# The integer additions of the weight conversion in a two-layer kernel: on GpSimd or on VectorE

## Chip, cores and metric

The kernel runs on one core of a Trainium2 chip. The metric is the device time of one execution in microseconds (us), from the first to the last instruction and what lies around them. TensorE (PE in the profile, PEld for its weight loads), VectorE (DVE), ScalarE (ACT), GpSimd (POOL) and SyncE (SP, which issues most transfers) run side by side; each works through its own instructions in the order in which they stand, and semaphores make one wait for another.

## What is computed

An attention block over 2 x 768 tokens, a dense layer with an ELU between two matrix products, and a mixture of eight experts of which each token takes one. The change touches only the dense layer, which the code calls the first layer:

```python
def _moe_ref(x, w_in, w_out):            # x: 1536 x 512, w_in: 512 x 2048, w_out: 2048 x 512
    h = x @ w_in
    alpha = 1.0
    g = np.where(h > 0.0, h, alpha * (np.exp(np.minimum(h, 0.0)) - 1.0))
    return (g @ w_out).astype(np.float32)
```

`w_in` and `w_out` are handed to the kernel as 64-bit words (the bits of doubles), and the kernel itself makes 32-bit floats of them.

## The kernel before

**Tiling.** The 1536 tokens stand in 4 blocks of 512, 256, 384 and 384 (index `j`), and the 2048 hidden columns in 16 slices of 128 (index `c`, `NF = 16`). For each block and slice PE makes `h` (`mm_h`, L422: 12 matmuls, because each product of 128 x 128 is taken three times: upper half by upper half, upper by lower, lower by upper), ACT and DVE make the ELU of it (`elu`: ACT L433 to L435, DVE L436 and L437), ACT and DVE split the result into an upper and a lower half (`split_g`: ACT L447, DVE L448), and PE adds its share to `y` (`mm_y1`, L467). In block 0 the slices below `C3 = 8` take one full float32 product for `y` (rows `y<-wo,elp`); from slice 8 on it is three products of halves (`y<-wsp,gh` and `y<-wsp,gl`), which needs the weight's halves, from ACT L175 and DVE L176.

**The conversion** of one weight slice goes over three engines. DVE shifts and masks the upper words into the tile `cv_t` (`conv_t`, L138 and L139), ACT scales the lower words into `cv_r` (`conv_r`, L127), and `conv_f` (L146) adds the two as 32-bit integers: in place into `cv_t` for `w_in`, into `wo` for `w_out`. There are 32 slices (16 of `w_in`, 16 of `w_out`), so 32 such additions, all on GpSimd before. For `w_in` the result is then split: ACT rounds the upper half (`conv_h`, L152), and `conv_l` (L157) subtracts it to give the lower half `wi`. The table `LOE` puts slices 3, 9 and 15 of these subtractions on GpSimd and the other 13 on DVE.

**Attention beside it.** While block 0 runs through its slices, the attention of the tokens of block 1 is made in units of 64 tokens: scores on PE (L309), maximum on DVE (L319, L324), exponentials on ACT (L336), normalisation on DVE (L353, L354, L361), a transpose on PE (L371), a copy on ACT (L378), the product with the values on PE (L392), and its halves on ACT (L398) and DVE (L405). Transpose and product use one PSUM bank, `T`, of which there is only one: the transpose of the next unit waits until L405 of the unit before has read it.

**What sets the order.** Up to the first slices of block 0 the order is written out by hand (`START`, run by `start_up`): there `A`, `B` and `C` with a slice and a 0 (`w_in`) or 1 (`w_out`) are the conversion's three steps, `D` and `E` the halves. `START` holds seven of the 32 additions and the subtractions of slices 0 to 3. The rest comes from a loop over blocks and slices (in `part1`) with two conversions to each slice; there the Tile framework's own scheduler sets the order of the instructions on every engine. The tiles `cv_t` and `cv_r` come from one pool of 5 buffers (`stg`), the raw `w_out` slices from one of 4 (`ws`), so later loads wait for earlier conversions.

Of the kernel before, what the change touches and what calls it, by code (L numbers as in the profile page):

```python
# [9 lines left out]
F32 = mybir.dt.float32  # L10
# [5 lines left out]
ALU = mybir.AluOpType  # L16
# [40 lines left out]
EXD = (3, 5)  # L57
EXP = (0, 1, 2, 3, 4, 6, 7)
NORMD = (0, 4, 7)
LOE = "VVVPVV"  # L60
START = "w23 w43 x3 w53 w03 w13 w33 w51 x1 w31 w21 w11 w41 w01 w52 x2 w22 w02 w12 w42 w50 x0 w00 w20 w32 d2 d0 w40 d5 k2 s0 w30 d3 k4 k1 k3 s2 k0 k5 m0 w10 s5 m2 e0 s3 m5 M0 e2 m3 d4 M1 r0 b5 d1 b3 s4 n0 e5 r2 t0 e3 m4 n2 s1 c0 z3 e4 M2 z5 t2 r3 r5 M3 n3 c2 m1 A00 M4 n5 B00 e1 M5 k6 r4 C00 n4 t5 P s6 r1 c5 p1 n1 A01 p6 t4 p2 D0 o5 B01 c4 o2 h5 k7 m6 t3 C01 h2 s7 c3 E0 e6 t1 p7 m7 p0 A10 r6 o0 c1 p3 n6 p4 e7 o3 l5 B10 o1 t6 h3 r7 h0 C10 l3 c6 n7 o4 A11 l0 h1 t7 B20 h4 o6 A20 c7 l1 C20 h6 l4 o7 D1 l2 l6 H0 h7 E1 D2 l7 A30 B30 E2 C30 H1 B11 C11 D3 A21 B21 E3 C21"
HID = (5, 10, 15)
LOP = (1, 3, 5, 8, 10, 12, 14)
# [16 lines left out]
class Prog:  # L80
# [60 lines left out]
    def conv_f(self, c, part):  # L141
        t2, r = self.cv.pop((c, part))
        f = t2
        if part == 1:
            f = self.wo[:, c].bitcast(I32)
        self.nc.gpsimd.tensor_tensor(f, t2, r, op=ALU.add)  # L146
        self.w[c, part] = f

    def conv_h(self, c):
# [4 lines left out]

    def conv_l(self, c):
        w, f = self.w[c, 0], self.cvf.pop(c)
        (self.nc.gpsimd if LOE[c % len(LOE)] == "P" else self.nc.vector).tensor_tensor(w[:, 1], f, w[:, 0].bitcast(F32), op=ALU.subtract)  # L157

    def conv_a(self, c, part):
        self.conv_r(c, part)  # L160
# [376 lines left out]
    def part1(self):  # L537
# [31 lines left out]
        for x in ORDER.split():  # L569
            f = dict(q=self.load_q, n=self.load_v0, v=self.load_v, w=wload, k=self.load_k0, c=self.load_c)[x[0]]  # L570
            f(int(x[1:]))
        self.new_x(0)
        self.new_x(1)
        self.start_up()
        conv_done = [x for x in pieces if x in self.w]
        del cq[:len(conv_done)]
        while dq and dq[0] in self.split:
# [66 lines left out]
        for i in range(len(steps)):  # L644
            run(2 * i)
            j, c = steps[i]
# [19 lines left out]
    def start_up(self):  # L666

        unit = dict(d=self.diag_q, k=self.k_sum, s=self.scores, m=self.maxes, b=self.less_max, e=self.at1b, z=self.sums, r=self.recip, n=self.norm,
                    t=self.turn, c=self.turned, o=self.weighted, h=self.x_hi, l=self.at5, p=self.v_pad, x=self.max_k0, M=self.mean_v0)
        part = dict(A=self.conv_r, B=self.conv_t, C=self.conv_f)  # L670
        self.split, self.half = set(), set()
        with self.tc.manual_schedule():
            for op in START.split():
                if op[0] == "H":
                    self.mm_h(0, int(op[1:]), 0, TB // 2)
                    self.half.add(int(op[1:]))
                    continue
                k, n = op[0], [int(i) for i in op[1:]]
                if k in unit:
                    unit[k](*n)  # L680
                elif k in part:
                    part[k](*n)
                    if k == "C" and n[1] == 1:
                        self.split.add((n[0], 1))
                elif k == "w":
                    self.window(*n)
                elif k == "P":
                    self.pad_v0()
                elif k == "D":
                    self.conv_h(*n)  # L690
                elif k == "E":
                    self.conv_l(*n)
                    self.split.add((n[0], 0))
# [805 lines left out]
```

## Time and profile before

| | us |
|---|---|
| median of 3 runs (567.41 to 567.75) | 567.46 |
| the profiled execution | 567.08 |
| its span | 565.3 |
| PE busy over the span | 538.3 (95%) |
| DVE busy | 366.3 (65%) |
| ACT busy | 311.4 (55%) |
| POOL busy | 115.7 (20%) |

The profile's times start at the first instruction of the profiled execution; around its span lie 1.8 us more. Matmuls overlap in their records, so a matmul's cost is the distance between starts, not its duration. PEclk is the granted clock of TensorE as a share of 2.4 GHz. A DVE instruction's record also overlaps the next one's by about 0.08 us.

### The profile page before, as it was taken

The page shows a single profiled execution, that of the slowest core. Times are in us where ns is not written, and L with a number is a line of the kernel's source. Part 1 is how long each engine was busy: PE and PEld are TensorE (multiplying, and loading weights), DVE is VectorE, ACT ScalarE, POOL GpSimd, SP SyncE. Part 2 cuts the span into 40 slices and gives each one's busy share as a digit, 9 for nine tenths or more (in the row PEclk, how much of TensorE's full clock was granted, in tenths as well). Part 3 has the DMA queues.
Part 4 walks back from the last instruction along what each step waited for, and adds up shares of the span by engine and source line. Part 5 has one row for each costly group of instructions (what it writes and reads, how often), then busy time and mean ns, then how long its engine had stood idle before and what let it go on. Part 6 is the DMA issues. An engine that isn't in the chain of part 4 may idle for free. (4 is left out here: it accounts for less than half of the span.)

```text
span 565.3 us, 9614 instructions
## 1 busy us (share of the span) xinstructions
PE 538.3 (95%) x3113; PEld 422.5 (75%) x3113; DVE 366.3 (65%) x966; ACT 311.4 (55%) x768; POOL 115.7 (20%) x139
## 2 busy tenths in 40 slices
PE   8877998789999999999999999999999999999995
PEld 4465664557889888988888989877888665675884
DVE  6999899997647886787565778885741100444510
ACT  5775564546557877775665754673232222565620
POOL 3656365434000000000000000431432111100001
PEclk9979999889999999999999999998999999999999
DMA  9999733342114130310100101541077979593611
GB/s 291 317 353 399 239 139 105 123 133 52 57 48 138 49 93 16 118 48 14 48 2 1 56 1 50 170 118 56 19 221 267 382 260 370 162 379 131 237 56 40
DMA packets 38714, 81.33 MB, mean 144 GB/s; under 512 B 4095, under 2 KB 8575, under 8 KB 38656
## 3 DMA queue, kind: packets, MB, share of 16 engines
q1 hardware_dynamic: 36336, 73.30, 38.8%
q0 software_dynamic: 2320, 7.34, 3.8%
q8 instruction: 26, 0.43, 0.3%
q14 instruction: 32, 0.26, 0.1%
HBM read 103.70 MB, written 6.55 MB: 195 GB/s over the span
## 5 line engine op out<-in xcount | busy, mean ns | idle before, releaser
L422 PE MATMUL h<-xh,wi 128*128 128x384 f32 (+2 forms) x528 | 144.6, 342 | 0.2 <-ACT elp L435 0.2
L467 PE MATMUL y<-wsp,gh 128*128 128x512 f32 x320 | 100.9, 403 | 0.3
L422 PEld LDWEIGHTS h<-xh,wi 128*128 128x128 f32 x528 | 93.6, 189 | 8.3 <-ACT elp L435 1.0
L422 PE MATMUL h<-xl,wi 128*128 128x384 f32 (+2 forms) x264 | 88.0, 333 | 0.0
L467 PEld LDWEIGHTS y<-wsp,gh 128*128 128x128 f32 x320 | 58.2, 191 | 10.5 <-ACT gh L447 1.1
L467 PE MATMUL y<-wsp,gl 128*128 128x512 f32 x160 | 62.3, 405 | 1.3 <-DVE gl L448 1.3
L1157 DVE TENSOR_TENSOR holdl<-S,holdh 128x512 fp32r<-128x512 f32 x22 | 15.2, 689 | 72.1 <-ACT holdh L1153 53.7
L1125 PE MATMUL h<-w2s,holdh 128*128 128x512 f32 x176 | 61.0, 407 | 0.0
L1168 PE MATMUL y<-w2s,holdh 128*128 128x512 f32 x176 | 59.1, 398 | 0.0
L436 DVE SCALAR_TENSOR_TENSOR elt<-ele,elt 128x384 f32<-128x384 f32 (+2 forms) x64 | 41.3, 646 | 19.5 <-ACT ele L434 19.1
L422 PEld LDWEIGHTS h<-xl,wi 128*128 128x128 f32 x264 | 49.9, 189 | 4.5 <-issue 1.2
L433 ACT ACTIVATE elt<-h 128x384 f32<-128x384 f32 (+2 forms) x64 | 31.4, 491 | 28.5 <-PE h L422 23.0
L447 ACT CAST gh<-elp 128x384 fp32r<-128x384 f32 (+2 forms) x56 | 27.8, 496 | 31.9 <-DVE elp L437 22.0
L176 DVE TENSOR_TENSOR wsp<-wo,wsp 128x512 fp32r<-128x512 f32 x56 | 39.9, 713 | 8.2 <-ACT wsp L175 7.5
L437 DVE SCALAR_TENSOR_TENSOR elp<-elt,elp 128x384 f32<-128x384 f32 (+2 forms) x64 | 41.8, 652 | 3.9
L175 ACT CAST wsp<-wo 128x512 fp32r<-128x512 f32 x56 | 34.7, 620 | 15.4 <-PE y L467 13.8
L1125 PEld LDWEIGHTS h<-w2s,holdh 128*128 128x128 f32 x176 | 33.9, 192 | 8.3 <-issue 0.8
L336 ACT ACTIVATE e<-e,nb 128x120 f32<-128x120 f32 x88 | 33.7, 389 | 10.4 <-DVE nb L324 10.2
L1168 PEld LDWEIGHTS y<-w2s,holdh 128*128 128x128 f32 x176 | 33.1, 188 | 8.4 <-issue 1.6
L448 DVE TENSOR_TENSOR gl<-elp,gh 128x384 fp32r<-128x384 f32 (+2 forms) x56 | 31.0, 554 | 12.1 <-ACT gh L447 10.8
L467 PEld LDWEIGHTS y<-wsp,gl 128*128 128x128 f32 x160 | 29.9, 190 | 8.4 <-DVE gl L448 2.5
L1125 PE MATMUL h<-w2s,holdl 128*128 128x512 f32 x88 | 35.0, 398 | 0.0
(290 smaller groups left out, 973.1 us busy)
## 6 DMA issues: line engine op xcount, KB each, us to landing
wo<-in_w SPq DMA_DIRECT2D x9, 2048.0 KB
wo<-in_w SPq DMA_DIRECT2D x18, 1024.0 KB
ri<-in_w_in SPq DMA_DIRECT2D x16, 512.0 KB
ro<-in_w_out SPq DMA_DIRECT2D x16, 512.0 KB
wo<-in_w SPq DMA_DIRECT2D x32, 256.0 KB
w2p<-in_w SPq DMA_DIRECT2D x32, 256.0 KB
w2q<-in_w SPq DMA_DIRECT2D x24, 256.0 KB
q<-in_q SPq DMA_DIRECT2D x18, 256.0 KB
```

Of the source, the lines that this page charges most:

```text
L175: nc.scalar.copy(w[:, 0], f)
L176: nc.vector.tensor_tensor(w[:, 1], f, w[:, 0].bitcast(F32), op=ALU.subtract)
L336: nc.scalar.activation(e[:, p], e[:, p], AF.Exp, bias=nb[:, p:p + 1], scale=0.125, accum_out=sm[:, p:p + 1])
L422: nc.tensor.matmul(h, lhsT=w[:, wl, k * 128:k * 128 + 128], rhs=x[:, k, a:b], start=(n == 0), stop=(n == 11))
L433: nc.scalar.activation(t, h, AF.Tanh, scale=0.5)
L436: nc.vector.scalar_tensor_tensor(t, e, 1.0, t, op0=ALU.add, op1=ALU.mult)
L437: nc.vector.scalar_tensor_tensor(p, t, 0.0, p, op0=ALU.min, op1=ALU.add)
L447: nc.scalar.copy(gh, p)
L448: nc.vector.tensor_tensor(gl, p, gh.bitcast(F32), op=ALU.subtract)
L467: nc.tensor.matmul(self.y[j][t], lhsT=gx[:, sl], rhs=wx, start=(c == 0 and n == 0), stop=(c == NF - 1 and n == len(ops) - 1))
L1125: nc.tensor.matmul(self.h[s, hf], lhsT=x[:, k], rhs=w, start=(n == 0), stop=(n == 11))
L1168: nc.tensor.matmul(self.y2[s], lhsT=g[:, ks], rhs=w, start=(i == 0 and n == 0), stop=(i == 7 and n == 2))
```

## The change

The table `LOE` goes, and `conv_l` always stands on VectorE. `conv_f` asks a flag, `self.early`, that is set while `start_up` runs and cleared behind it: the seven additions of `START` stay on GpSimd, the other 25 go to VectorE. The subtractions of slices 3 (in `START`), 9 and 15 go to VectorE too. So 28 instructions move.

```diff
@@ -57,7 +57,6 @@
 NORMD = (0, 4, 7)
-LOE = "VVVPVV"
...
@@ -143,7 +142,7 @@
         f = t2
         if part == 1:
             f = self.wo[:, c].bitcast(I32)
-        self.nc.gpsimd.tensor_tensor(f, t2, r, op=ALU.add)
+        (self.nc.gpsimd if self.early else self.nc.vector).tensor_tensor(f, t2, r, op=ALU.add)
         self.w[c, part] = f
...
     def conv_l(self, c):
         w, f = self.w[c, 0], self.cvf.pop(c)
-        (self.nc.gpsimd if LOE[c % len(LOE)] == "P" else self.nc.vector).tensor_tensor(w[:, 1], f, w[:, 0].bitcast(F32), op=ALU.subtract)
+        self.nc.vector.tensor_tensor(w[:, 1], f, w[:, 0].bitcast(F32), op=ALU.subtract)
...
@@ -572,6 +571,7 @@
         self.start_up()
+        self.early = False
         conv_done = [x for x in pieces if x in self.w]
...
@@ -668,7 +668,7 @@
-        self.split, self.half = set(), set()
+        self.split, self.half, self.early = set(), set(), True
```

Since one line goes, L60 to L571 of the kernel before are one lower in the changed one: its L145 is L146 here. The scheduler also sets many instructions behind `start_up` in another order, on PE, DVE, ACT and SP. Three places follow.

GpSimd, from the end of `START` on, before (`cv_t` and `wo` are additions, `wi_655` is the lower half of slice 3, L297 copies key maxima for the attention, L709 prepares routing constants):

```order
L709 CAST wg_668<-r_wg_670 128x4x16
L146 TENSOR_TENSOR cv_t<-cv_t,cv_r 128x512
L146 TENSOR_TENSOR wo<-cv_t,cv_r 128x512
L157 TENSOR_TENSOR wi_655<-cv_t,wi_655 128x512
L146 TENSOR_TENSOR wo<-cv_t,cv_r 128x512
L297 COPY k<-ks_96 128x96
```

and in the changed kernel:

```order
L709 CAST wg_668<-r_wg_670 128x4x16
L145 TENSOR_TENSOR cv_t<-cv_t,cv_r 128x512
L145 TENSOR_TENSOR wo<-cv_t,cv_r 128x512 x2
L296 COPY k<-ks_96 128x96 x2
L296 COPY k<-ks_97 128x96 x12
L1199 TENSOR_TENSOR w2s<-wo,w2s 128x512 x3
```

Behind the additions of `START` no conversion is left on GpSimd; only the small copies of L297 stand there until the experts' weights.

VectorE around the first ELU instructions of block 0, before:

```order
L437 SCALAR_TENSOR_TENSOR elp<-elt,elp 128x512
L138 TENSOR_SCALAR cv_t<-ri_701 128x512
L324 TENSOR_SCALAR nb<-mx 128x4
L139 SCALAR_TENSOR_TENSOR cv_t<-ri_701,cv_t 128x512
L436 SCALAR_TENSOR_TENSOR elt<-ele,elt 128x512
L437 SCALAR_TENSOR_TENSOR elp<-elt,elp 128x512
```

and in the changed kernel:

```order
L137 TENSOR_SCALAR cv_t<-ri_701 128x512
L436 SCALAR_TENSOR_TENSOR elp<-elt,elp 128x512
L145 ISA wo<-cv_t,cv_r 128x1024
L323 TENSOR_SCALAR nb<-mx 128x4
L138 SCALAR_TENSOR_TENSOR cv_t<-ri_701,cv_t 128x512
L435 SCALAR_TENSOR_TENSOR elt<-ele,elt 128x512
L145 ISA cv_t<-cv_t,cv_r 128x1024
```

The additions stand between the conversion's first step and the ELU. On VectorE they have another form: a custom instruction (ISA) that sees the same 512 words of a partition as 1024 elements of two bytes.

TensorE at the end of `h` of slice 8 (`wi_1013`) and at the turn of an attention unit, before:

```order
L422 MATMUL h<-xl_202,wi_1013 128x512
L371 MATMUL T<-c_128,e 120x128 x4
L422 MATMUL h<-xh_201,wi_1013 128x512
L309 MATMUL S<-k,q 128x120 x4
L467 MATMUL y<-wo,elp 128x512 x4
```

and in the changed kernel:

```order
L421 MATMUL h<-xl_202,wi_1013 128x512
L421 MATMUL h<-xh_201,wi_1013 128x512
L308 MATMUL S<-k,q 128x120 x4
L370 MATMUL T<-c_128,e 120x128 x4
L466 MATMUL y<-wo,elp 128x512 x4
```

The transpose into the bank `T` (L371) stands two steps later, behind the scores of the next unit.

## Rows read from the trace of the kernel before

**Rows 1.** The page's head.
```profile
span 565.3 us, 9614 instructions
```

**Rows 2.** Windows: length, busy us (instructions) by engine, PEclk, DMA share, GB/s.
```profile
47.07:140.37 93.30, 81.11 (x348) 53.24 (x346) 87.07 (x152) 52.34 (x119) 45.30 (x33) 0.95 0.48 160
140.37:200.00 59.63, 59.63 (x432) 52.40 (x431) 41.11 (x116) 40.77 (x116) 2.42 (x5) 1.00 0.24 77
200.00:300.00 100.00, 100.00 (x702) 89.44 (x701) 72.02 (x245) 68.41 (x202) 1.73 (x5) 1.00 0.14 43
```

**Rows 3.** Waits of PE, 47.07 to 140.37: total us, times, longest.
```profile
PE T L371 <- DVE xl L405: 5.5, 2, 4.4
PE y L467 <- DVE elp L437: 3.2, 1, 3.2
PE y L467 <- DVE gl L448: 1.3, 1, 1.3
PE T L392 <- ACT et L378: 1.1, 1, 1.1
```

**Rows 4.** Timeline of PE: start, us, instruction, [idle before <- releaser].
```profile
53.24 5.37 PE L467 MATMUL y<-wo,elp 128*128 128x512 f32 x8 [3.16 <-DVE elp L437]
...
61.21 3.59 PE L467 MATMUL y<-wo,elp 128*128 128x512 f32 x8
...
101.28 0.65 PE L371 MATMUL T<-c,e 128*120 128x128 f32 x4 [4.40 <-DVE xl L405]
```

**Rows 5.** Timeline of POOL.
```profile
93.26 1.27 POOL L146 TENSOR_TENSOR cv_t<-cv_t,cv_r 128x512 int32<-128x512 int32 x1 [0.72 <-DVE rr L353]
94.48 1.48 POOL L157 TENSOR_TENSOR wi<-cv_t,wi 128x512 fp32r<-128x512 f32 x1
```

**Rows 6.** Timeline of DVE at the same time.
```profile
93.30 1.51 DVE L138 TENSOR_SCALAR cv_t<-ro 128x512 int32<-128x512 int32 x1
94.73 1.75 DVE L361 TENSOR_TENSOR e<-e,rr 128x480 f32<-128x480 f32 x1
```

**Rows 7.** DVE groups, 47.07 to 140.37: xcount | busy us, mean ns | idle before.
```profile
L437 DVE SCALAR_TENSOR_TENSOR elp<-elt,elp 128x512 f32<-128x512 f32 x12 | 14.4, 1202 | 0.5
L157 DVE TENSOR_TENSOR wi<-cv_t,wi 128x512 fp32r<-128x512 f32 x10 | 12.7, 1267 | 0.0
L436 DVE SCALAR_TENSOR_TENSOR elt<-ele,elt 128x512 f32<-128x512 f32 x12 | 12.5, 1045 | 0.8 <-ACT ele L434 0.6
...
L139 DVE SCALAR_TENSOR_TENSOR cv_t<-ri,cv_t 128x512 int32<-128x512 int32 x12 | 9.8, 818 | 0.0
L138 DVE TENSOR_SCALAR cv_t<-ro 128x512 int32<-128x512 int32 x13 | 9.5, 734 | 3.2 <-POOL wi L157 3.2
L138 DVE TENSOR_SCALAR cv_t<-ri 128x512 int32<-128x512 int32 x12 | 5.0, 416 | 0.0
L361 DVE TENSOR_TENSOR e<-e,rr 128x480 f32<-128x480 f32 x4 | 4.8, 1193 | 0.0
```

**Rows 8.** DVE groups, 200 to 300, where GpSimd is nearly idle.
```profile
L176 DVE TENSOR_TENSOR wsp<-wo,wsp 128x512 fp32r<-128x512 f32 x23 | 15.9, 689 | 3.6 <-ACT wsp L175 3.3
...
L361 DVE TENSOR_TENSOR e<-e,rr 128x480 f32<-128x480 f32 x8 | 5.2, 656 | 0.2
...
L448 DVE TENSOR_TENSOR gl<-elp,gh 128x256 fp32r<-128x256 f32 x9 | 3.8, 422 | 0.7 <-ACT gh L447 0.6
```

**Rows 9.** POOL groups, 47.07 to 140.37.
```profile
L146 POOL TENSOR_TENSOR wo<-cv_t,cv_r 128x512 int32<-128x512 int32 x14 | 20.4, 1455 | 20.8 <-DVE cv_t L139 8.6 <-ACT wi L152 4.5 <-issue 3.4
L146 POOL TENSOR_TENSOR cv_t<-cv_t,cv_r 128x512 int32<-128x512 int32 x12 | 18.9, 1578 | 20.1 <-DVE cv_t L139 8.2 <-ACT cv_r L127 5.9 <-ACT wsp L175 3.5
L157 POOL TENSOR_TENSOR wi<-cv_t,wi 128x512 fp32r<-128x512 f32 x3 | 4.5, 1506 | 0.7 <-ACT wi L152 0.7
```

**Rows 10.** Timeline of DVE while GpSimd rests.
```profile
131.79 0.68 DVE L139 SCALAR_TENSOR_TENSOR cv_t<-ri,cv_t 128x512 int32<-128x512 int32 x1
132.39 0.67 DVE L448 TENSOR_TENSOR gl<-elp,gh 128x512 fp32r<-128x512 f32 x1
```

## Prediction

> **What bounds the kernel now.** I read three views, from wide to narrow. First the windows [rows 2]: from 140 us on TensorE is busy for 59.63 of 59.63 us and then for 100.00 of 100.00, at the full granted clock of 2.4 GHz. It is the bound there, so whatever an earlier stage ends sooner arrives at the end of the kernel. The stage of 47 to 140 us, the slices 2 to 12 of the first block, is another matter: in 93.3 us TensorE is busy for 81.11, so it stands still for 12.2 us, and at a granted clock of 0.95; VectorE is busy for 87.07.
>
> Second, the waits of TensorE in that stage [rows 3]. Three of the four groups end on VectorE (5.5, 3.2 and 1.3 us); the fourth, 1.1 us, is for a ScalarE copy. GpSimd ends none of the long ones itself. In the timeline the two largest are seen singly [rows 4]: 3.16 us before the first `y` of the block, and 4.40 us before a transpose that needs the bank `T`, which VectorE's L405 had still to read. After the first wait the clock is down, too: the same product takes 5.37 us there and 3.59 us eight microseconds later.
>
> Third, why VectorE is late. At 93.26 us GpSimd starts an addition and at 94.48 a subtraction, which ends at 95.96 [rows 5]. VectorE's mask operation of 93.30 lasts 1.51 us, to 94.81, and its normalisation of 94.73 lasts 1.75, to 96.48 [rows 6], although these forms take 0.416 (mean of the undisturbed group) and 0.656 us elsewhere [rows 7, 8]. Each ends some 0.3 to 0.5 us behind GpSimd's. So a VectorE instruction that meets a GpSimd one stands until that one is done: VectorE is full, but not of its own work.
>
> **The change part by part.** *Removed from VectorE: the standing.* The cost is read from the groups of the stage against undisturbed means [rows 7, 8], 0.689 us for a form with two operands of 512 elements. L437: 12 x (1.202 - 0.689) = 6.2 us; L157: 10 x (1.267 - 0.689) = 5.8; L436: 12 x (1.045 - 0.689) = 4.3; L138 on `ro`: 13 x (0.734 - 0.416) = 4.1; L361: 4 x (1.193 - 0.656) = 2.1; L139 on `ri`: 12 x (0.818 - 0.689) = 1.5. Together 24.0 us. GpSimd has 29 conversion instructions in the stage [rows 9]; one addition of `START` stays and 28 go, so 24.0 x 28/29 = 23.2 us are freed. The copies of L297 stay and are short.
>
> *Added to VectorE: 25 additions and 3 subtractions.* A subtraction is the form of L157, which follows its predecessor at 0.60 us when nothing disturbs it, as two instructions of that size do (131.79 to 132.39) [rows 10]. The addition is not in the trace; in the changed order it is a custom form over 1024 two-byte elements. Bounds from rows: 0.60 us if it goes by bytes, since it reads and writes exactly what a subtraction of 512 words does; and if it goes by elements, (0.689 - 0.422) / 256 = 1.04 ns each [rows 8], so 0.689 + 512 x 1.04 ns = 1.22 us, less the 0.08 of overlap 1.14. I take 0.60, because L139 on `ri`, an integer form over the same tiles, costs what the float forms cost (0.68 us) [rows 10]; 1.14 is kept for a rival. Sum added: 28 x 0.60 = 16.8 us.
>
> The Trainium skill's page VectorE: DVE Perf Modes (section on the perf-mode tier table) says that `tensor_tensor` runs at one element a cycle on fp32 and at two on 16-bit operands. If the custom form follows the 16-bit row, an addition of 1024 elements takes 0.69 us by that page's figures and the sum stays as it is; if it follows the fp32 row, 1.22 us, which is the rival below. No row here shows which.
>
> *VectorE's demand* in the stage then is 87.1 - 23.2 + 16.8 = 80.7 us. The order takes some of it out: four of the 25 additions and two subtractions now stand behind the ELU of slice 11, which ended this stage before, 6 x 0.60 = 3.6 us, leaving 77.1. They fall into the window after 140 us, where VectorE has 59.6 - 41.1 = 18.5 us free [rows 2].
>
> *TensorE's demand.* Busy 81.1 us at a clock of 0.95; at the full clock 81.1 x 0.05 = 4.1 us less, 77.0. The first wait I leave where it is: the operations ahead of it lose a little standing and gain a subtraction and a mask operation. It costs 3.2 us and 5.37 - 3.59 = 1.8 us of clock. So TensorE needs 77.0 + 5.0 = 82.0 us, against 77.1 for VectorE: TensorE becomes the bound of the stage too. The transpose of the 4.40 us wait also stands later on TensorE now, behind the scores, which gives L405 more time.
>
> *What the move costs in waits.* An addition on VectorE now holds up all behind it (the next ELU, the lower halves of `x` and `g`) while it waits for ScalarE's `cv_r`. VectorE's spare of 82.0 - 77.1 = 4.9 us covers that in part, and TensorE has up to one slice of work in hand; I book 1 us of new waits. On SP the loads of raw `w_out`, of key sums and of values now wait for VectorE's additions in place of GpSimd's; they are wanted much later, and DMA is busy for 0.48 of the stage, so they cost nothing. GpSimd itself has nothing else to do there but L297.
>
> *Sum:* 93.3 - 82.0 = 11.3 us gained, less 1.0: 10.3. The profiled execution took 567.08 us for a span of 565.3 [rows 1], so around the span lie 1.8 us that do not change; the median of the runs is 0.4 us above it. From the median: 567.46 - 10.3 = 557.2 us.
>
> **The rivals.** *A, the addition goes by elements.* VectorE's demand is 87.1 - 23.2 + 25 x 1.14 + 3 x 0.60 = 94.2 us; four additions and two subtractions fall behind the stage (5.8), 88.4 are left, with 2 us of waits 90.4. VectorE stays the bound and the gain is 93.3 - 90.4 = 2.9: 564.5 us. For it: the element count in the order. Against it: the bytes. This is what the one-element-a-cycle row of the page named above would give.
>
> *B, the waits move with the work: slower.* GpSimd's waits that were not for VectorE are 4.5 + 3.4 + 5.9 + 3.5 + 0.7 = 18.0 us [rows 9]: for ScalarE, and "issue". On GpSimd they cost little; if all of them come to stand in VectorE's queue, with the 3.0 us that it idles now for others than GpSimd (93.3 - 87.1 - 3.2), the stage takes 77.1 + 3.0 + 18.0 = 98.1 us, 4.8 longer: 572.3 us. It decides from 93.3 - 77.1 - 3.0 = 13.2 us of such waits on, 0.47 us to each moved instruction. Against it: ScalarE is busy for only 52.3 of 93.3 us [rows 2], and much of its own idling is for the conversion's additions and subtractions, which come sooner now; and the scheduler sets two conversions' mask operations ahead of their additions.
>
> *C, given back later: no change.* The reordered first block ends sooner, but the left-over conversions and the ELU of block 1 then meet on VectorE and TensorE waits there for as long: 567 us. Against it: 18.5 us free for 3.6 us of work.
>
> That the change does not do what it says is no case: the changed order has no conversion on GpSimd behind `START`.
>
> **How the numbers follow.** The forecast, TensorE as the bound of the stage, gets 0.72; A 0.13; B 0.09; C 0.06. A measurement of this kernel can tell 0.2%, 1.1 us, from no change. Faster by more than that are the forecast and A, 0.85, less 0.01 for an A that comes out dearer: 0.84. Within it C, 0.06. Slower B, and the dearer A, 0.10. The range: below, the whole of TensorE's loss goes but a part of the first wait, 12.2 + 4.1 - 1.3 = 15.0 us: 552.5. Above, A's 564.5 as a whole, so that B and C alone lie outside it, 0.15.
>
> **What would show it.** Right: in 47 to 140 us the groups L437, L436 and L157 fall to means of 0.7 to 0.75 us; the additions on VectorE stand with 0.69 us; the wait for L405 is gone or under 1 us; the windows show TensorE full for the slices 3 to 12 at a clock near 1.00; slice 13 starts at 127 to 130 us and not at 140. The first wait stays near 3 us. Wrong: additions of 1.2 us (A); VectorE idle by 13 us or more with "ACT cv_r" as the releaser (B); idle TensorE between 130 and 200 us (C). The step I trust least is the 1 us of new waits: with TensorE and VectorE within 5 us of each other for the whole stage, a few badly placed instructions cost more than that.

## The result, and the profile after

The changed kernel takes **552.96 us** (median of 4 runs, 551.34 to 554.55) beside 567.43 us before (567.31 to 567.75) on the same chip: a ratio of 0.9744, 95% interval 0.9712 to 0.9775, so 14.5 us faster. Forecast were 557.2 us with a range of 552.5 to 564.5, so the time lies 4.2 us under the forecast and 0.5 us inside the range. A second comparison gave 553.17 us and 0.9747 (0.9719 to 0.9775). Ratios leave disturbed executions out, so for two of the experiments below (`e3_gpsimd_reads_again` and `e6_second_addition`) the ratio says less time than the median does, and the profile of the first, which is of a disturbed execution, is not read.

The profiled execution took 552.2 us for a span of 550.4, so 1.8 us lie around the span, as before. Line numbers from L60 to L571 are one lower than before: L435 and L436 after are L436 and L437 before, L145 is L146, L156 is L157.

To see where 14.9 us of span went I cut both traces at the same three pieces of TensorE work: up to the first product `h` of the first layer, from there to its last, and the rest. The windows of the kernel before, in the columns of [rows 2] (length, busy PE, PEld, DVE, ACT, POOL, then the granted clock):

```profile
40.25:376.35 336.10, 323.89 (x1975) 269.41 (x1974) 266.64 (x680) 214.19 (x551) 64.25 (x55) 0.98 0.29 94
376.35:565.30 188.95, 181.79 (x884) 132.21 (x883) 64.93 (x158) 69.21 (x124) 30.57 (x39) 0.98 0.56 196
```

The same of the kernel after, and below it its first layer cut once more, at the point where TensorE has as much left to do as it had before at 140.37 us (14.57 + 221.40 = 235.97 us busy, against 235.96 before):

```profile
39.54:363.15 323.61, 319.21 (x1975) 267.82 (x1973) 258.81 (x708) 215.52 (x551) 24.09 (x27) 0.99 0.30 98
363.15:550.40 187.25, 179.78 (x884) 131.13 (x883) 64.41 (x158) 68.63 (x123) 30.08 (x39) 0.99 0.56 197
...
47.07:125.80 78.73, 76.25 (x340) 50.99 (x341) 73.85 (x172) 51.11 (x117) 4.53 (x5) 0.98 0.54 181
125.80:140.37 14.57, 14.57 (x78) 12.41 (x77) 13.90 (x34) 10.66 (x27) 0.59 (x2) 1.00 0.26 84
140.37:363.15 222.78, 221.40 (x1502) 197.61 (x1501) 163.62 (x495) 149.37 (x400) 14.37 (x17) 1.00 0.19 60
```

The layer is 336.10 - 323.61 = 12.5 us shorter: TensorE's idle time in it fell from 12.2 to 4.4 us, and its busy time, on the same products, from 323.9 to 319.2 us. The layer also starts 0.7 us sooner, and the rest of the kernel is 1.7 us shorter. The stage of [rows 2] went from 93.30 to 78.73 us; VectorE's busy time in it from 87.07 to 73.85.

What TensorE still waits for, from the layer's first product to its last (total us, times, longest):

```profile
PE y L466 <- DVE elp L436: 2.5, 1, 2.5
PE y L524 <- ACT mab L511: 1.4, 1, 1.4
PE h L421 <- ACT elp L434: 0.5, 1, 0.5
```

The waits for L405 and L448 of [rows 3] are gone, the first wait, 3.2 us there, is 2.5 us here, and 1.4 us for a ScalarE copy are new, at 166 to 167 us. In the stage itself the first wait is all that is left: 78.73 - 76.25 = 2.48 us. The VectorE groups of 44 to 140 us, which answer to [rows 7]:

```profile
L138 DVE SCALAR_TENSOR_TENSOR cv_t<-ro,cv_t 128x512 int32<-128x512 int32 x15 | 11.2, 749 | 0.1
L435 DVE SCALAR_TENSOR_TENSOR elt<-ele,elt 128x512 f32<-128x512 f32 x15 | 10.4, 690 | 2.3 <-ACT ele L433 2.3
L436 DVE SCALAR_TENSOR_TENSOR elp<-elt,elp 128x512 f32<-128x512 f32 x15 | 10.3, 683 | 0.1
L145 DVE CUSTOM_DVE_ANT_0 wo<-cv_t,cv_r 128x1024 uint16<-128x1024 uint16 x13 | 8.9, 682 | 0.4 <-ACT cv_r L126 0.4
L156 DVE TENSOR_TENSOR wi<-cv_t,wi 128x512 fp32r<-128x512 f32 x13 | 8.8, 679 | 0.2 <-ACT wi L151 0.2
L137 DVE TENSOR_SCALAR cv_t<-ro 128x512 int32<-128x512 int32 x15 | 8.5, 566 | 0.0
...
L145 DVE CUSTOM_DVE_ANT_0 cv_t<-cv_t,cv_r 128x1024 uint16<-128x1024 uint16 x12 | 8.2, 680 | 0.0
```

The three groups that stood at 1202, 1045 and 1267 ns stand at 683, 690 and 679. The addition, L145, costs 0.68 us, as much as a subtraction. Its waits for ScalarE come to 0.4 us.

### The profile page after: what moved, and what is told of

Its sections match the earlier page's. It is cut to its first block, busy times and chain, and to the rows that moved or that the text cites. A ratio compares the mean times of both kernels' runs of the same rounds, so it can differ in the third digit from the quotient of the medians.

```text
span 550.4 us, 9589 instructions
## 1 busy us (share of the span) xinstructions
PE 528.4 (96%) x3113; PEld 417.6 (76%) x3113; DVE 357.8 (65%) x994; ACT 312.5 (57%) x768; POOL 74.2 (13%) x111
## 5 line engine op out<-in xcount | busy, mean ns | idle before, releaser
L466 PE MATMUL y<-wsp,gh 128*128 128x512 f32 x320 | 98.5, 398 | 0.1
L466 PE MATMUL y<-wsp,gl 128*128 128x512 f32 x160 | 60.5, 399 | 0.0
L1125 PE MATMUL h<-w2s,holdh 128*128 128x512 f32 x176 | 59.8, 400 | 0.0
L435 DVE SCALAR_TENSOR_TENSOR elt<-ele,elt 128x384 f32<-128x384 f32 (+2 forms) x64 | 37.1, 580 | 23.8 <-ACT ele L433 23.5
L436 DVE SCALAR_TENSOR_TENSOR elp<-elt,elp 128x384 f32<-128x384 f32 (+2 forms) x64 | 35.5, 554 | 3.2
L296 POOL COPY k<-ks 128x96 f32<-128x96 f32 x16 | 8.2, 516 | 199.3 <-PE S L308 137.6
L1168 PE MATMUL y<-w2s,holdl 128*128 128x512 f32 x88 | 34.4, 391 | 0.0
```

Source lines behind the costliest of these rows:

```text
L435: nc.vector.scalar_tensor_tensor(t, e, 1.0, t, op0=ALU.add, op1=ALU.mult)
L436: nc.vector.scalar_tensor_tensor(p, t, 0.0, p, op0=ALU.min, op1=ALU.add)
L466: nc.tensor.matmul(self.y[j][t], lhsT=gx[:, sl], rhs=wx, start=(c == 0 and n == 0), stop=(c == NF - 1 and n == len(ops) - 1))
L1125: nc.tensor.matmul(self.h[s, hf], lhsT=x[:, k], rhs=w, start=(n == 0), stop=(n == 11))
L1168: nc.tensor.matmul(self.y2[s], lhsT=g[:, ks], rhs=w, start=(i == 0 and n == 0), stop=(i == 7 and n == 2))
```

## The experiments

Two theories stand against each other. *Standing*: a GpSimd instruction that reads its operands holds up a VectorE instruction that reads two, so every conversion step on GpSimd costs VectorE time although it relieves it. *Relief or order*: VectorE does better for other reasons, because the planner now orders the block in another way, or because the few subtractions were badly placed. In the kernels that add work, nothing is left out: the added instructions write a scratch tile that nobody reads.

**The changed kernel once more**, beside the kernels below.

> The changed kernel once more, timed against the one before on one chip with the three kernels below. Standing theory: a gain of 13 to 15 us as measured before, with the same stage of 47 to 126 us: TensorE busy for 76 us, VectorE for 74. What is open is the granted clock of the 30 to 40 us stretch, 1.00 in the first profile of the changed kernel and 0.69 in the one before: if it was luck, it is about 0.7 here, and the first matmul of the layer starts 0.7 us later, with the total some 1 us longer.

Measured 553.17 us (551.99 to 554.93), 0.9747 (0.9719 to 0.9775). Its first layer is 324.86 us long in the profile, 1.3 more than the first trace has; so differences of 1 to 2 us between two single profiles are not explained here. The clock of 30 to 40 us is 1.00 again, not about 0.7; yet the layer starts at 40.35 us, as late as in the kernel before. So the 0.7 us by which it starts sooner in the first trace are not the change's.

**The change in two halves.** The first keeps three subtractions of the first block on GpSimd and moves only the additions; the second starts from the kernel before and moves only the subtractions.

The lines that differ in where an instruction runs:

```diff
--- after
+++ e1_additions_only
-        self.nc.vector.tensor_tensor(w[:, 1], f, w[:, 0].bitcast(F32), op=ALU.subtract)
+        (self.nc.gpsimd if c % 6 == 3 else self.nc.vector).tensor_tensor(w[:, 1], f, w[:, 0].bitcast(F32), op=ALU.subtract)
--- before
+++ e2_subtractions_only
-        (self.nc.gpsimd if LOE[c % len(LOE)] == "P" else self.nc.vector).tensor_tensor(w[:, 1], f, w[:, 0].bitcast(F32), op=ALU.subtract)
+        self.nc.vector.tensor_tensor(w[:, 1], f, w[:, 0].bitcast(F32), op=ALU.subtract)
```

> The changed kernel with the subtractions of slices 3, 9 and 15 back on GpSimd; the 25 additions stay on VectorE. Standing theory (a VectorE instruction that meets a GpSimd one stands until it is done, and that was what the change removed): three such meetings come back, about 1 us each, less 0.6 us of work each, and VectorE has spare, so 553 to 556 us. Order theory (the gain comes from the scheduler's other order of PE and VectorE): the order differs from the changed kernel's in some 200 lines on PE, so anything from 553 to 567.

> The kernel before with only the three subtractions moved to VectorE; all 32 additions stay on GpSimd. Standing theory: 3 of 28 meetings go, 2.5 us of standing against 1.8 us of added work, so 564 to 568 us, and the groups L436, L437, L157 keep means near 1.0 to 1.2 us. Order theory: the order on PE differs from that before in 251 lines, nearly as many as the changed kernel's, so a good part of the 14.5 us could come: 555 to 562.

Measured: the additions alone 554.11 us, 0.9754 (0.9714 to 0.9794), not to be told from the whole change; the subtractions alone 563.37 us, 0.9931 (0.9906 to 0.9955), 4 us, of which its profile has 2.1 us in the layer and 2.4 behind it. That is somewhat more than the standing theory gave, and the means of L435, L436 and L156 in 47 to 140 us are 828, 897 and 791 ns there, where 1.0 to 1.2 us were expected. So the additions carry the gain, and beside them the three subtractions are worth no more than the intervals leave open. Why the subtractions alone give little is in the waits of TensorE in that kernel, from 36 us on:

```profile
PE T L370 <- DVE xl L404: 3.6, 2, 3.1
PE y L466 <- DVE gl L447: 3.4, 2, 1.8
PE y L466 <- DVE nb L323: 3.2, 1, 3.2
```

VectorE still ends three long waits: 25 additions are left on GpSimd to meet it.

**GpSimd's reads put back, in the changed order.** Behind each of the 13 `w_out` additions that now run on VectorE, GpSimd makes two, or one, needless additions on the result; or, in the third kernel, six memsets, which read nothing, behind a copy of one column. The order of the other engines is the changed kernel's.

```diff
+        if part == 1 and not self.early:
+            for _ in range(2):      # e3; range(1) in e7
+                self.nc.gpsimd.tensor_tensor(self.scr, self.wo[:, c], self.wo[:, c], op=ALU.add)
```
```diff
+        if part == 1 and not self.early:      # e4
+            self.nc.gpsimd.tensor_copy(self.scr[:, :1], self.wo[:, c, :1])
+            for _ in range(6):
+                self.nc.gpsimd.memset(self.scr, 0.0)
```

> The changed kernel, with 26 needless additions on GpSimd (two behind each addition of a w_out slice; each reads 512 floats twice and writes a scratch tile that nobody reads). The order on PE, VectorE, ACT and SP is word for word the changed kernel's. Standing theory: each holds VectorE for 0.8 to 1.0 us, some 20 to 26 us in the stage of 47 to 126 us, where VectorE is busy for 73.9 of 78.7 us, so VectorE becomes the bound again: 563 to 573 us, and the means of L436, L437 and L157 (by the lines of before) rise to 0.9 to 1.2 us. Order theory: nothing waits for these instructions, so 552 to 555 us.

> The changed kernel with 13 needless additions on GpSimd, one behind each moved addition of a w_out slice; the order on PE, VectorE, ACT and SP is the changed kernel's. Standing theory: 13 meetings of 0.6 to 1.0 us, 8 to 13 us on VectorE, of which some 5 us find spare: 555 to 561 us, half of the way back to the kernel before. Order theory: 552 to 554 us.

> The changed kernel, with 78 needless memsets on GpSimd (six behind each addition of a w_out slice, behind a copy of one column), some 35 to 40 us of GpSimd's time as in the kernel before; a memset reads nothing. The order on PE, VectorE, ACT and SP is word for word the changed kernel's. Standing by GpSimd's reads: VectorE's two-operand instructions don't stand, only the one-operand mask operation (L138 of before) may, so 553 to 557 us with two-operand means near 0.69 us. Standing by whatever GpSimd runs: 563 to 573 us, as with the needless additions.

Measured ratios: 26 reads 0.9895 (0.9836 to 0.9953), 13 reads 0.9902 (0.9872 to 0.9933), 78 memsets 0.9854 (0.9797 to 0.9911). So 26 reads cost 0.0151 x 567 = 8.6 us against the changed kernel, 13 cost 8.8, and the memsets 6.2. By time alone the three don't tell reading from writing, nor one dose from two: by these ratios the 26 reads, at 561 us, stay under the range of the standing theory, the 13 reads stand at its upper end, and the memsets, at 559 us, lie above theirs. VectorE's busy time in the layer is 264.02 us with 13 reads and 261.30 with the memsets, against 258.81. But the added work brought a second thing with it, which I had not thought of: TensorE now waits for the key copies of the layer (L296 after, on GpSimd). In the kernel with 13 reads:

```profile
PE S L311 <- POOL k L299: 3.2, 1, 3.2
```
```profile
126.65 5.96 POOL L299 COPY k<-ks 128x96 f32<-128x96 f32 x2 [0.48 <-PE y L469]
```

The two copies start 0.48 us behind the needless addition ahead of them, and then they take 5.96 us, against 2.26 us for the same two in the changed kernel (from 123.56 us on), where the median of one is 0.27 us. From 126.45 to 132.28 us VectorE goes without a gap from one two-operand instruction to the next, with one mask operation among them; the copies end 0.33 us behind that. With the memsets the two copies take 3.55 us, and TensorE waits for 2.0. These three settle nothing on the time, and were done again without that wait, below.

**VectorE's spare.** The changed kernel with a second, needless addition on VectorE behind each of the 25 moved ones.

```diff
+        if not self.early:
+            self.nc.vector.tensor_tensor(self.scr, f.bitcast(F32), f.bitcast(F32), op=ALU.add)
```

> The changed kernel with a needless second VectorE addition of 512 floats (into a scratch tile) behind each of the 25 moved ones, 0.60 us each, so 15 us more work for VectorE: what an addition that goes by elements would have cost. Spare theory (the stage ends with TensorE, and VectorE, busy for 73.9 of 78.7 us, has some 4.8 us of spare): 10 us of it reach the end: 560 to 564 us. If VectorE is not near the bound at all: 553 us.

Measured 0.9949 (0.9909 to 0.999), so 0.0202 x 567 = 11.5 us more than the changed kernel, for 25 x 0.60 = 15.0 us of work. Single executions lie far apart, from 560.67 to 571.25 us; the profiled one took 568.57. Its layer:

```profile
40.12:378.37 338.25, 326.11 (x1976) 271.74 (x1973) 271.16 (x733) 215.03 (x552) 29.00 (x29) 0.97 0.29 95
```

VectorE is busy for 271.2 us, 12.4 more than in the changed kernel, and the layer is 2 us longer than in the kernel before, with 29.0 us of GpSimd's work in it where the kernel before had 64.3. So VectorE has little to spare: had an addition cost about twice 0.60 us (the first rival), most of the gain would have gone. But not all of the loss is the length of VectorE's own work. Here, too, TensorE waits for two key copies that take 6.47 us while VectorE works without a gap (from 133.39 to 139.82 us), although GpSimd has no added work in this kernel:

```profile
133.69 6.47 POOL L298 COPY k<-ks 128x96 f32<-128x96 f32 x2 [67.15 <-DVE ks L223]
```
```profile
140.00 2.06 PE L310 MATMUL S<-k,q 128*128 128x120 f32 x8 [3.35 <-POOL k L298]
```

**All of it on VectorE.** First the seven additions of `START`, then the sixteen key copies as well.

```diff
--- after
+++ e5_all_on_vector
-        (self.nc.gpsimd if self.early else self.nc.vector).tensor_tensor(f, t2, r, op=ALU.add)
+        self.nc.vector.tensor_tensor(f, t2, r, op=ALU.add)
--- e5_all_on_vector
+++ e8_key_copies_too
-            self.nc.gpsimd.tensor_copy(k[:, 0], self.ks[u // UPB])
+            self.nc.vector.tensor_copy(k[:, 0], self.ks[u // UPB])
```

> The changed kernel with the seven additions of START on VectorE too. Standing theory: seven meetings fewer before 50 us, up to 7 us of standing against 4.2 us of work, in a stretch where VectorE is busy for 9.2 to 9.9 of each 10 us; the first matmul of the layer (39.5 us) starts 0 to 2 us sooner: 551 to 553 us. Rival (the exception was needed): the additions hold up the attention's own work in VectorE's queue while they wait for ScalarE, and the layer starts 1 to 4 us later: 554 to 557 us.

> The kernel of e5_all_on_vector again, as the partner of e8_key_copies_too: 549 to 553 us.

> The kernel after with START's seven additions and the sixteen key copies (L296 there) on VectorE as well, so that GpSimd has nothing of the first layer's first block behind START. If GpSimd's remaining part still costs anything: 549 to 552 us, and no wait of TensorE on k from GpSimd. If the copies cost VectorE more than they free (16 copies of 0.2 us and a changed order): 553 to 555 us.

Measured 551.2 us (0.9716, 0.9684 to 0.9747) and, again, 551.66 us (0.9735, 0.9712 to 0.9759) for the first, which the intervals don't set apart from the changed kernel. With the key copies 549.99 us (548.84 to 551.28), 0.97 (0.9677 to 0.9724): by the ratios about 2.5 us less than the changed kernel (0.9744 and 0.9747), though the intervals still touch. TensorE waits for no key copy there. GpSimd has nothing left in 47 to 200 us there, and two groups that were still stretched in the changed kernel have come down, L138 on `ro` from 749 and L137 on `ro` from 566 ns (44 to 140 us):

```profile
L138 DVE SCALAR_TENSOR_TENSOR cv_t<-ro,cv_t 128x512 int32<-128x512 int32 x15 | 10.3, 689 | 0.0
...
L137 DVE TENSOR_SCALAR cv_t<-ro 128x512 int32<-128x512 int32 x14 | 5.9, 426 | 0.5 <-DMA ro<-in_w_out 0.5
```

**Reads and writes once more, with nothing else on GpSimd.** The last kernel is the ground for the clean form of the test: two needless additions behind each of the 13, or six memsets, by the same edits as above. The order of the other engines is that of `e8_key_copies_too`, and no other instruction of that stretch is on GpSimd.

> The kernel of e8_key_copies_too with 26 needless GpSimd additions, two behind each w_out addition, that read SBUF; the order of the other engines is as there, and nothing waits for GpSimd. The standing theory: VectorE's busy time in the first layer grows by 15 to 17 us, the two-operand groups from 0.68 to 0.75 to 1.0 us, and the time by 6 to 13 us. The rival, that the first such experiment was slow through the key copies that queued behind the additions (a wait of 4.1 us): the time grows by at most 4 us.

> The same with 78 GpSimd memsets, six behind each w_out addition, which write SBUF and read nothing (a copy of one column ahead of each six apart). The standing theory: the two-operand groups stay at 0.68 us, VectorE's busy time in the first layer grows by 2 to 4 us, all of it in the mask operations, and the time by at most 3 us. The rival, that GpSimd's work as such costs time (through the clock, say): the time grows by 6 us or more, as in the first such experiment, with the clock of 126 to 200 us under 0.97.

Measured: 26 reads 559.06 us (557.33 to 560.31), 0.9859 (0.9837 to 0.9881), 9 us more than their ground; 78 memsets 550.44 us (548.39 to 551.51), 0.9703 (0.968 to 0.9727), not to be told from it. GpSimd is the busier in the second: 52.84 us in the layer with the reads, 70.14 with the memsets. The layers of the ground, of the reads and of the memsets:

```profile
39.58:358.83 319.25, 317.94 (x1974) 266.65 (x1973) 257.38 (x725) 215.31 (x551) 10.38 (x8) 1.00 0.30 98
```
```profile
38.97:368.59 329.62, 320.93 (x1976) 267.44 (x1973) 275.12 (x727) 214.70 (x551) 52.84 (x36) 0.99 0.29 97
```
```profile
40.79:360.95 320.16, 317.39 (x1974) 266.32 (x1973) 260.05 (x725) 215.75 (x551) 70.14 (x99) 1.00 0.30 99
```

On the same instructions VectorE is busy for 17.7 us more with the reads (0.68 us for each; 15 to 17 us were expected) and 2.7 us more with the memsets, nearly all of it in the mask operation (15 x 0.097 + 12 x 0.089 = 2.5 us). Some of the groups of 44 to 140 us with the reads, then with the memsets:

```profile
L145 DVE CUSTOM_DVE_ANT_0 cv_t<-cv_t,cv_r 128x1024 uint16<-128x1024 uint16 x12 | 10.8, 899 | 0.0
L438 DVE SCALAR_TENSOR_TENSOR elt<-ele,elt 128x512 f32<-128x512 f32 x13 | 10.6, 814 | 0.0
```
```profile
L439 DVE SCALAR_TENSOR_TENSOR elt<-ele,elt 128x512 f32<-128x512 f32 x15 | 10.2, 682 | 0.2
...
L145 DVE CUSTOM_DVE_ANT_0 cv_t<-cv_t,cv_r 128x1024 uint16<-128x1024 uint16 x13 | 8.8, 681 | 0.0
...
L137 DVE TENSOR_SCALAR cv_t<-ro 128x512 int32<-128x512 int32 x15 | 7.8, 523 | 1.2 <-DMA ro<-in_w_out 1.1
```

With the reads four further two-operand groups stand at 719 to 747 ns, and `gl` at 850; the additions into `wo`, behind which the reads start, and `wsp` are undisturbed (682 and 684). One meeting in the kernel with the reads, in the timelines of POOL and of DVE:

```profile
79.31 2.78 POOL L148 TENSOR_TENSOR scr<-wo 128x512 bf16<-128x512 f32 x2 [2.55 <-issue]
```
```profile
79.67 1.52 DVE L438 SCALAR_TENSOR_TENSOR elt<-ele,elt 128x512 f32<-128x512 f32 x1
81.12 1.52 DVE L145 CUSTOM_DVE_ANT_0 cv_t<-cv_t,cv_r 128x1024 uint16<-128x1024 uint16 x1
```

Two GpSimd additions, ending at 82.09; two VectorE instructions of 0.68 us beside them take 1.52 each, the second until 82.64, 0.55 us behind GpSimd's end. It is the pattern of [rows 5, 6], made at will. That sets the standing theory apart from order and relief: the order is the same in all three kernels, and so is what VectorE has to do. It does not say how the 14.5 us are shared. The largest wait of the kernel before, for L405 (5.5 us in [rows 3]), does not come back with the reads, neither here nor with the 13 reads above, and the transpose that had it stands later in the changed kernel's order. So how much of the gain is the new order's own stays open.

The Trainium skill's page SBUF — State Buffer (section Who interferes with whom) states that a VectorE instruction with two SBUF inputs contends with a GpSimd instruction that reads SBUF, not with one that only writes it. The last pair of kernels agrees: 682 and 681 ns beside memsets, 814 and 899 beside additions. The same page of the Trainium skill (section Summary: rules for kernel authors) states that of two such instructions the second one to issue fully blocks until the first finishes. The meeting above agrees: GpSimd's addition of 79.31 us starts first, and VectorE's instruction of 79.67 takes 0.84 us longer than its 0.68.

Why the memsets cost 6 us in the first form and none in the second is seen in the first layer of `e4_gpsimd_writes_only`, which is 5.6 us longer than the changed kernel's. TensorE waits there for 2.0 us for the key copies, and behind that wait its clock is down for 8 us:

```profile
132.00:134.00 2.00, 2.00 (x12) 1.73 (x11) 1.43 (x10) 0.00 (x0) 1.28 (x3) 0.72 0.17 36
134.00:136.00 2.00, 2.00 (x9) 1.90 (x9) 2.00 (x6) 0.61 (x2) 1.77 (x5) 0.50 0.94 319
136.00:138.00 2.00, 2.00 (x6) 1.52 (x6) 0.71 (x2) 0.24 (x1) 1.21 (x2) 0.50 0.01 5
138.00:140.00 2.00, 2.00 (x7) 1.57 (x6) 0.00 (x0) 0.14 (x1) 0.00 (x0) 0.57 0.00 0
```

That is worth (0.28 + 0.50 + 0.50 + 0.43) x 2 = 3.4 us of full-speed work; with the wait, 5.4 of the 5.6 us. In the second form no key copy is on GpSimd. That GpSimd's work as such lowers TensorE's clock, the rival named ahead of that run, is not borne out: with the memsets and nothing else the clock is 1.00 over the layer.

## Why the prediction was right, and where its sizes were off

*TensorE is the bound behind the stage* held: what the layer gained (12.5 us) arrived at the end. TensorE idles for 222.78 - 221.40 = 1.4 us in the rest of the layer, so the third rival (given back later) fell but for these 1.4 us.

*VectorE stands when it meets GpSimd* held, and was then shown for two-operand instructions and GpSimd's reads. That TensorE's waits are mostly for VectorE held as well; the view of [rows 3] has two more, of 0.9 us for L405 and 0.2 us for ScalarE, so it is four groups of six and not three of four. Over the layer VectorE's busy time fell by 266.64 - 258.81 = 7.8 us, where the forecast had 23.2 freed - 16.8 added = 6.4. With the additions at the forecast price 24.6 us were freed.

*The addition costs 0.60 us* held: its groups stand at 0.68 us, with the usual overlap of 0.08. The first rival (1.14 us, by elements) fell. On the page VectorE: DVE Perf Modes of the Trainium skill, which the forecast had left open, it is the 16-bit rate of `tensor_tensor` in the perf-mode tier table that agrees with 0.68 us (0.69 us by that page, as estimated in the prediction).

*VectorE's demand of 77.1 us in the stage* came out as 73.85: more work than forecast now stands ahead of the stage (7.43 us busy in 39.54 to 47.07, against 6.6 before) and behind it (13.90 + 163.62 = 177.5, against 41.11 + the rest, 172.95 before: 4.6 us more, 3.6 forecast), and 24.6 us were freed instead of 23.2. So TensorE was the bound by a wider margin than 4.9 us, and the moved waits found room: 0.4 us for `cv_r`, where the second rival needed 13.2 us of such waits. It fell.

*TensorE's idle time.* Forecast 3.2 us for the first wait and 1 us of new ones, 8.0 us less than before; measured 4.4 us, 7.8 less. The parts were off and cancel, which is luck: the first wait is 2.5 us for 3.2, and the new waits are 1.9 us (0.5 and 1.4) for 1.0. None of the others for VectorE is left. The step I trusted least was off by 0.9 us.

*The clock is the term that was mis-sized.* The forecast took 81.1 x 0.05 = 4.1 us from the mean clock of the stage and gave 1.8 back for the first wait, 2.3 net. Busy time in the layer fell by 4.7. The mean hid that the loss hangs on single waits. In the kernel before, windows of 2 us:

```profile
54.00:56.00 2.00, 2.00 (x4) 0.79 (x3) 1.75 (x3) 2.00 (x9) 1.67 (x1) 0.57 1.02 399
56.00:58.00 2.00, 2.00 (x3) 0.73 (x3) 2.00 (x6) 2.00 (x6) 0.12 (x1) 0.58 1.08 256
...
102.00:104.00 2.00, 2.00 (x10) 1.99 (x9) 1.97 (x4) 0.99 (x2) 0.84 (x2) 0.51 0.00 0
104.00:106.00 2.00, 2.00 (x4) 0.73 (x4) 2.00 (x3) 0.67 (x1) 0.81 (x1) 0.63 0.69 193
...
122.00:124.00 2.00, 1.32 (x5) 1.24 (x6) 2.00 (x5) 0.00 (x0) 0.00 (x0) 0.63 0.03 8
124.00:126.00 2.00, 2.00 (x6) 1.60 (x5) 2.00 (x3) 0.00 (x0) 1.54 (x2) 0.51 0.16 24
```

Each stretch stands behind waits: the first two behind the 3.16 and the 4.40 us of [rows 4], the third behind 1.27 and 1.11 us that lie close together. Each is worth (1 - 0.57 + 1 - 0.58) x 2 = 1.7 us of full-speed work, 5.1 in all, a little less where TensorE also idled. After, one is left, behind the first wait:

```profile
52.00:54.00 2.00, 1.53 (x2) 0.84 (x3) 2.00 (x5) 1.59 (x4) 0.00 (x0) 0.58 1.03 407
54.00:56.00 2.00, 2.00 (x4) 0.80 (x3) 2.00 (x5) 2.00 (x10) 0.00 (x0) 0.57 1.04 371
```

Two of three went, 3.4 us. Counted by waits the forecast would have been 1.1 us nearer. Of the other 1.3 us of busy time 0.2 is the head of the layer, where the kernel before had a clock of 0.76 from 40.25 to 41 us; the rest I can't place.

*What lies outside the layer* was left at nothing. In this profile it gave 0.7 us ahead and 1.7 behind. I don't count these as the change's. The layer of `e0_changed_again` starts at 40.35 us, and the last part is 186.6 us in `e2_subtractions_only` and 189.0 in `e5_all_on_vector`, at clocks of 0.99 and 0.98, in no order that fits their edits. In sum: 7.8 + 4.7 + 0.7 + 1.7 = 14.9 us of span, against 8.0 + 2.3 = 10.3 forecast. It is these 2.4 us, which the forecast has no mechanism for, and the clock that bring the time so near to the lower end of the range.

*The signs.* The forecast's groups (0.7 to 0.75 us) came out at 0.68 to 0.69, the wait for L405 is gone, the clock is 0.98 over the stage and 1.00 from 56 us on. Slice 13 can't be compared, since the order of the products changed; in its place stands the cut at equal work, 125.80 us for 140.37, sooner than the 127 to 130 us given for it.

## What to carry to other kernels

Before work is given to GpSimd to relieve VectorE, look at the means of VectorE's two-operand groups with GpSimd busy and with it idle: here each GpSimd addition of 512 elements cost VectorE 0.68 us, more than the 0.60 us that the addition costs on VectorE itself, so the relief was none. If GpSimd must work beside a full VectorE, let it write without reading. Look at GpSimd's side as well: two short copies that TensorE needed took about 6 us here beside a VectorE that never paused. And price a wait of TensorE with the clock behind it: in the kernel before, the waits of 3.16 and 4.40 us, and two of 1.27 and 1.11 us close together, cost another 1.7 us each time, while a wait of 1.14 us by itself (for L378, at 111 us) cost none; in `e4_gpsimd_writes_only` a wait of 1.95 us cost 3.4.

## What I had not expected of the hardware

- A one-operand VectorE form, the mask L137, is stretched by GpSimd too, and by memsets as well as by additions: on `ro` 426 ns with GpSimd idle, 523 beside memsets, 732 beside additions (mean of 44 to 140 us; the last from the kernel `e9_reads_nothing_else`). The two-operand forms are held up by the additions, which read, and not by the memsets.
- GpSimd stands as well, as the key copies of `e7_gpsimd_reads_half` and `e6_second_addition` show. Its copy of a single column in `e10_writes_nothing_else` took 4.87 us at 78.13, where the median of the 13 such copies is 0.53. VectorE worked without a gap meanwhile, all but two of its instructions with two operands, and the copy ended 0.12 us after VectorE went over to the masking of scores, which reads PSUM:

```profile
78.13 4.87 POOL L147 CAST scr<-wo 128x1 bf16<-128x1 f32 x1
```
```profile
82.28 0.68 DVE L145 CUSTOM_DVE_ANT_0 wo<-cv_t,cv_r 128x1024 uint16<-128x1024 uint16 x1
82.88 0.27 DVE L322 CUSTOM_DVE_ANT_0 e<-S,mask 128x120 f32<-128x120 f32 x1
```

- In the changed kernel the start-up ran at a clock of 1.00 from 30 to 40 us in both profiles, where the kernel before had 0.69, and yet the layer began only 0.7 us sooner in one and no sooner in the other: TensorE idles there for 4.5 us in the first, against 2.9 before. The kernels with work added to the changed one have the same order there and clocks of 0.70 (`e4_gpsimd_writes_only`, `e7_gpsimd_reads_half`), so I can't put the clock down to the change.
